# A new written-out order for all engines, with 44 constant matmuls in place of 30

## The chip, the core and the metric

The kernel runs on one NeuronCore of a Trainium2 chip. The core has five engines that work side by side, each through its own instructions in order: TensorE (PE, matmuls and transposes; its weight loads are shown apart as PEld), VectorE (DVE), ScalarE (ACT), GpSimd (POOL) and SyncE (SP, which here only issues DMA transfers). POOL issues DMA transfers too, those that convert to another type on the way. The metric is the device time of one execution in microseconds (us); lower is better.

## The reference

A block-sparse attention feeds a gated feed-forward layer. There are 4 batches, 8 heads, 768 positions and 64 dimensions; keys are cut into 24 chunks of 32, and every query keeps the 6 chunks with the highest upper bound.

```python
k_min = np.min(k_chunks, axis=3)
k_max = np.max(k_chunks, axis=3)
ub = np.sum(np.maximum(q[:, :, :, None, :] * k_min[:, :, None, :, :], q[:, :, :, None, :] * k_max[:, :, None, :, :]), axis=-1)
ub = np.where(causal, ub, -1000000000.0)
top_chunks = np.argsort(ub, axis=-1)[..., -top_k:]
scores = scale * np.matmul(q, k.transpose(0, 1, 3, 2))
scores = np.where(mask, scores, -1000000000.0)
...
attn = attn / (np.sum(attn, axis=-1, keepdims=True) + 1e-09)
return np.matmul(attn, v).astype(np.float32)
...
x = np.ascontiguousarray(attn_out.transpose(0, 2, 1, 3)).reshape(B * S, H * D)
gate = 1.0 / (1.0 + np.exp(-(x @ w_gate)))
val = x @ w_val
return (gate * val @ w_out).astype(np.float32)
```

The feed-forward layer has 512 inputs, 1536 hidden columns and 3072 tokens.

## The kernel before

**Units.** Tokens are worked in eight units of up to three blocks of 128 positions. Unit 0 holds the first block of batches 0, 1 and 2, which need no choice of chunks (they see only themselves); its three attentions are the small functions with an `f` in the name (`kfT_0`, `scf_1`, `pvf_2_0` and so on, the number being the batch). Unit 1 is blocks 1 to 3 of batch 0; units 2 to 7 follow.

**Steps of a first block** (`first`, from L699): load `k`, `q`, `v` in halves (`kf0_0`, `qf1_0`, `vf_0`, L636 and L631); transpose keys and queries on TensorE in f32 (`kfT`, `qfT`, L709); cast them to f16 (`kf16`, `qf16`, L454 on DVE, L452 on ACT); scores (`scf`, L746); two exponentials, one for each half of the heads (`expf`, ACT, L751); two causal masks on POOL (`cmf`, L753); values (`pvf`, L760, whose `v` was cast by `v16_0_0` or `vc`); reciprocal and scale on DVE (`rzf`, `xf`, L766 and L768); transpose back (`xpsf`, L775) and copy into the layer's input (`xTf`).

**Steps of unit 1** before its scores: load (`k0_u1` to `q3_u1`, L647); copy to a transposable layout (`kn`, `qn`); transpose (`kT`, `qT`, L795); chunk extremes (`kx0`, `kx1`, L681) and their difference (`kcr`, L688); copies of keys and queries into the score operands (`kt`, `hk`, `qf`, `hq`) and the clipped queries (`qm`, L695). The bounds are one group of matmuls (`ub_u1`, L896), which needs all of `kcr`, `qf` and `qm`. DVE then finds the sixth largest bound (`ubn`, `mx`, `ap`, `apt`), and `hqm` copies the resulting mask rows into the score operand. Rows of a fixed pattern (`epat`, copied by the eight `hkp`) stand opposite to them. The scores of unit 1 are `sc_u1_HEAD_BANK`.

**The layer.** `g_uN_I` and `v_uN_I` are the gate and value products of 128 hidden columns (four matmuls of 384 columns each, L1259); `tanh` (ACT) and `hg` (DVE) follow, then the output product (`o`, or the seven products `p1` to `p7` of a Strassen step, L1082). Weights come in three parts each by POOL's DMA queue with a cast from f32 to f16: `wg0` to `wg2` (L612), `wv0` to `wv2` (L613), `wo0` to `wo2` (L618). The first quarter of `wg0`'s rows is a transfer of its own, `wgp` (L610). A gate product of the first four hidden blocks reads both `wg0` and `wgp`.

**The constant matmuls.** `keep_awake` (L589 to L593) multiplies a tile of ones by itself into a PSUM bank that nobody reads. They are named `fl_0` to `fl_29`. Each writes a bank, so it takes its turn with the other users of that bank.

**What sets the order.** The functions above only describe operations. Three long strings give the rest. `ORDER` (from L96) lists all 2010 operations as `name=engine`; the kernel emits them in that order, and each engine (P, A, V, G for POOL, S for SP) runs its own in the order of the list. `SLOTS` gives the place of every rotating buffer: eight PSUM banks, six landing places for `kf`, `qf`, `vf` and the `v` loads, and so on. A transfer into a place waits until the old contents have been read. `TIES` adds waits that no data asks for: `a<b` makes `a`, always work of POOL, wait for the end of `b`, always work of DVE.

```python
        for w in ORDER.split():
            name, _, e = w.partition("=")
            op = ops[name]
            op.engine = {"P": PE, "A": ACT, "V": DVE, "G": POOL, "S": SP}[e]
...
        for b in ties.get(op.name, ()):
            tc.add_manual_dep(traced[n], ends[b], mybir.DependencyInfo(mybir.DependencyClass.Sync, mybir.DependencyReason.DATA), reason="tie")
```

Of the kernel before, what the change touches and what calls it, by code (L numbers as in the profile page):

```python
# [112 lines left out]
hk0_u1_0=A hq1_u1_1=A sc_u1_0_2=P exp_u1_0_2=A sc_u1_1_2=P sc_u1_0_1=P sc_u1_0_0=P exp_u1_1_2=A sc_u1_1_0=P sc_u1_1_1=P
exp_u1_0_0=A exp_u1_0_1=A v_u0_7=P wo0=G hqm0_u1_2=G sc_u1_2_2=P exp_u1_2_2=A sc_u1_2_0=P exp_u1_2_0=A sc_u1_3_0=P sc_u1_3_2=P
exp_u1_3_2=A exp_u1_1_0=A sc_u1_3_1=P exp_u1_3_1=A exp_u1_3_0=A v16_0_3=G wo1=G v_u0_4=P sc_u1_2_1=P v_u0_6=P exp_u1_2_1=A
hk1_u1_0=G v16_0_2=G wo2=G mx1_u1=V ap1_u1=V apt1_u1=V hqm1_u1_0=V g_u0_5=P tanh_u0_5=A v_u0_5=P exp_u1_1_1=A hqm1_u1_2=A g_u0_6=P
tanh_u0_6=A g_u0_7=P tanh_u0_7=A hg_u0_7=V v16_0_1=G cm_u1_3=G pv_u1_3=P cm_u1_2=G hk1_u1_1=G g_u0_4=P tanh_u0_4=A hg_u0_4=V
vf1_3=G hq1_u1_2=G pv_u1_2=P sc_u1_5_1=P sc_u1_4_2=P sc_u1_4_1=P rz_u1_1=V x_u1_1=V exp_u1_4_1=A v_u0_9=P v_u0_10=P xps_u1_1=P
xT_u1_1=A exp_u1_4_2=A hg_u0_6=V hk1_u1_3=V hg_u0_5=V v_u0_8=P g_u0_10=P tanh_u0_10=A kcr1=V hg_u0_10=V g_u0_8=P tanh_u0_8=A
hg_u0_8=V sc_u1_5_2=P exp_u1_5_2=A g_u0_9=P tanh_u0_9=A hg_u0_9=V sc_u1_4_0=P exp_u1_4_0=A cm_u1_1=G pv_u1_1=P cm_u1_0=G qn_u2_2=G  # L120
# [1336 lines left out]
```

## Time and profile before

| | us |
|---|---|
| Median of three runs | 281.13 |
| Lowest and highest | 280.3, 281.24 |
| The profiled execution | 279.88 |
| Its span, first to last instruction | 278.2 |
| PE busy | 269.2 |
| DVE, ACT, POOL busy | 231.2, 180.4, 163.1 |

The profile is of one execution. PE, DVE, ACT and POOL are busy times, and a busy TensorE is not TensorE at its peak, because the ends of matmuls are modelled. L numbers are lines of the kernel before. In a list in order of time each row has its start, its length, the engine, the line, the operation, what it writes and reads, and how many are merged (x); a bracket tells how long the engine stood idle before and what released it. A row of the waits has the time in total, the count and the longest. "PEclk" is the clock that TensorE was granted, and the DMA share is that of 16 engines, so that a value over 1 means that packets queue on them.

### The profile page before, as it was taken

Reading aid. Unit: us, or ns where it says so; the run is one execution under the profiler, and the core shown is the slowest. Engines: PE = TensorE matmul, PEld = TensorE weight load, DVE = VectorE, ACT = ScalarE, POOL = GpSimd, SP = SyncE. Lnnn points to the kernel's source line nnn. Section 1 sums busy time; section 2 is a strip of 40 time slices with the busy share of each in tenths; the row PEclk is TensorE's granted clock in tenths of the full one; section 3 lists DMA queues with packets and bytes.
Section 4 is the critical chain, followed back from the end, with each engine's and each line's share of the span. In section 5 each row is a group of like instructions: output and inputs, shape, how many; then the busy total and the mean of one; then the engine's idle time right before and its main releaser. Section 6 shows DMA issues by size and latency. Waiting matters only on the chain.

```text
span 278.2 us, 7566 instructions
## 1 busy us (share of the span) xinstructions
PE 269.2 (97%) x2806; PEld 189.3 (68%) x2806; DVE 231.2 (83%) x686; ACT 180.4 (65%) x386; POOL 163.1 (59%) x262
## 2 busy tenths in 40 slices
PE   5979999999999999999999999999999999999995
PEld 3755658667755666557687657776888688778684
DVE  4799747687999998796999987978889998888985
ACT  6388969569858944468689979988983422341430
POOL 5797744639372873534669966724766467163440
PEclk9999999999999999999999999999999999999999
DMA  6999999999999598696896230100320033000304
GB/s 157 258 281 204 207 217 208 220 179 202 187 217 189 142 183 188 145 161 125 164 157 114 68 85 17 40 0 3 73 77 2 1 83 127 2 1 2 151 2 152
DMA packets 131717, 34.70 MB, mean 125 GB/s; under 512 B 119776, under 2 KB 128736, under 8 KB 131680
## 3 DMA queue, kind: packets, MB, share of 16 engines
q1 hardware_dynamic: 126912, 29.50, 50.6%
q0 software_dynamic: 4768, 4.72, 10.1%
q8 instruction: 22, 0.36, 0.5%
q14 instruction: 15, 0.12, 0.1%
HBM read 30.67 MB, written 6.29 MB: 133 GB/s over the span
## 4 chain that ended last, share of the span: by engine, by line
PE 87%; DMA 6%; DVE 5%; SPq 1%; issue 0%; POOL 0%; DVEq 0%
PE v_u L1259 20%; PE g_u L1259 15%; PE sc_u L957 12%; PE o_u L1308 11%; PE p_u L1082 10%; PE pv_u L990 7%; DMA wg<-in_moe_w_gate_dram 5%; PE p_g_u L1191 5%; PE ube_u L896 3%; DMA kf<-in_k_dram 1%; DVE xf L768 1%; PE kfT L709 1%; PE qfT L709 1%; PE fl L591 1%; DVE kx_u L681 1%; DVE kcr L681 1%
## 5 line engine op out<-in xcount | busy, mean ns | idle before, releaser
L968 ACT ACTIVATE att_u<-sc_u 128x512 f16<-128x512 f32 (+3 forms) x184 | 86.9, 573 | 8.6 <-PE sc_u L957 7.3
L1259 PE MATMUL v_u<-xT_u,wv 128*128 128x384 f16 x384 | 72.4, 326 | 0.0
L1280 DVE SCALAR_TENSOR_TENSOR hg_u<-gate_u,v_u 128x384 f16<-128x384 f16 x96 | 51.2, 545 | 19.3 <-ACT gate_u L1271 9.7
L1271 ACT ACTIVATE gate_u<-g_u 128x384 f16<-128x384 f32 x72 | 35.1, 499 | 40.3 <-PE g_u L1259 35.1
L1259 PE MATMUL g_u<-xT_u,wg 128*128 128x384 f16 x288 | 56.0, 326 | 0.9 <-ACT xT_u L452 0.5
L1259 PEld LDWEIGHTS <-wv 128*128 128x128 f16 x384 | 36.2, 98 | 20.3 <-issue 0.2
L974 POOL TENSOR_SCALAR_AFFINE_SELECT att_u<-att_u 128x384 f16<-128x384 f16 (+1 forms) x56 | 28.0, 509 | 37.4 <-ACT att_u L968 16.4
L1259 PEld LDWEIGHTS <-wg 128*128 128x128 f16 x288 | 26.7, 98 | 18.3 <-DMA wg<-in_moe_w_gate_dram 1.8
L1308 PE MATMUL o_u<-wo,hg_u 128*128 128x512 f16 x144 | 34.3, 379 | 0.0
L990 PE MATMUL pv_u<-v,att_u 128*128 128x65 f16 x640 | 26.3, 193 | 0.0
L990 PEld LDWEIGHTS <-att_u 128*128 128x128 f16 x640 | 24.2, 98 | 2.9 <-issue 0.6
L1228 DVE TENSOR_TENSOR f_g_u<-p_g_u,f_g_u 128x192 f32<-128x192 f32 (+1 forms) x72 | 24.9, 383 | 1.0 <-PE p_g_u L1191 0.4
L957 PE MATMUL sc_u<-hqe,hke 128*128 128x128 f16 (+2 forms) x220 | 25.1, 243 | 0.0
L957 PE MATMUL sc_u<-hqo,hko 128*128 128x128 f16 (+2 forms) x220 | 24.1, 243 | 0.0
L1308 PEld LDWEIGHTS <-hg_u 128*128 128x128 f16 x144 | 13.7, 98 | 13.4
L957 PEld LDWEIGHTS <-hke 128*128 128x128 f16 x220 | 16.5, 98 | 4.9 <-issue 0.6
L957 PEld LDWEIGHTS <-hko 128*128 128x128 f16 x220 | 16.4, 98 | 4.4
L673 POOL CAST v<-v 128x512 f16<-128x512 f32 x23 | 14.4, 627 | 5.8 <-DVE qf_u L863 1.8
L1271 ACT ACTIVATE gate_u<-f_g_u 128x384 f16<-128x384 f32 x24 | 11.9, 519 | 5.6 <-DVE hg_u L1280 2.9
L1011 DVE TENSOR_TENSOR x_u<-pv_u,rz_u 128x384 f16<-128x384 f32 (+1 forms) x28 | 14.6, 524 | 0.9 <-DMA xT_u<-x_u 0.6
L919 DVE MAX8 mx_u<-ubn_u 128x8 f32<-128x8 f32 (+16 forms) x152 | 12.7, 158 | 0.3
L1099 DVE SCALAR_TENSOR_TENSOR sw<-p_u,sw 128x256 f32<-128x256 f32 (+1 forms) x20 | 10.6, 528 | 2.4 <-PE p_u L1082 2.0
(187 smaller groups left out, 504.9 us busy)
## 6 DMA issues: line engine op xcount, KB each, us to landing
v<-in_v_dram SPq DMA_DIRECT2D x23, 256.0 KB, 4.7
k<-in_k_dram SPq DMA_DIRECT2D x12, 384.0 KB, 5.4
q<-in_q_dram SPq DMA_DIRECT2D x12, 384.0 KB, 5.9
out_dram<-osb_u SPq DMA_DIRECT2D x12, 256.0 KB, 3.3
out_dram<-sw SPq DMA_DIRECT2D x8, 256.0 KB, 2.1
wv<-in_moe_w_val_dram POOLq DMA_DIRECT2D x3, 512.0 KB, 9.8
wo<-in_moe_w_out_dram POOLq DMA_DIRECT2D x3, 512.0 KB, 17.6
qf<-in_q_dram SPq DMA_DIRECT2D x8, 128.0 KB, 3.3
```

Source lines behind the costliest of these rows:

```text
L673: plan.add(f"v16_{b}_{ib}", {POOL: pool(H * D)}, lambda e: nc.gpsimd.tensor_copy(v16[b % 2][:, ib, :, 0:D], at(t)), reads=[t], writes=[("v ...
L957: nc.tensor.matmul(at(t)[:, o:o + 128 * m], hk[b % 2][e_][:, p, 128 * jb:128 * jb + 128], hq[u.side][e_][:, p, 128 * x:128 * (x + m)], sta ...
L968: plan.add(f"exp_{u.name}_{h}_{y}", {ACT: act(n)}, lambda e, t=t, att=att, b0=b0, n=n: nc.scalar.activation(at(att)[:, b0:b0 + n], at(t), ...
L974: nc.gpsimd.affine_select(out=dv, in_=dv, compare_op=ALU.is_ge, fill=0.0, base=0, pattern=[[0, u.m], [1, 128]], channel_multiplier=-1)
L990: nc.tensor.matmul(at(pv)[:, last, x, :], at(att)[:, c:c + 128], v16[b % 2][:, jb, h, :], start=(jb == 0), stop=(jb == ib))
L1011: plan.add(f"x_{u.name}_{p}", {DVE: dve(u.t)}, lambda e: nc.vector.tensor_tensor(at(x_).rearrange("p a (e d) -> p e a d", e=2), at(pv)[:, ...
L1082: nc.tensor.matmul(at(to)[:, side], a(j)[:, i], b(j)[:, i], start=j == i == 0, stop=j == 2 and i == 1)
L1228: plan.add(f"{p}_{name}", {POOL: pool2(192 * n), DVE: dve(192 * n)} if slow else {DVE: dve(192 * n)}, lambda e: both(e).tensor_tensor(dst( ...
L1259: nc.tensor.matmul(at(t), w16[:, c, 128 * fb:128 * fb + 128], at(u.xt)[:, c, :], start=(c == 0), stop=(c == 3))
L1271: plan.add(f"tanh_{u.name}_{fb}", {ACT: act(T, not seven[0])}, lambda e, gv=gv, gate=gate: nc.scalar.activation(at(gate), gv(), AF.Tanh, s ...
L1280: plan.add(f"hg_{u.name}_{fb}", {DVE: dve(T)}, lambda e, vv=vv, gate=gate, hg=hg, fb=fb: nc.vector.scalar_tensor_tensor(at(hg)[:, fb % 2], ...
L1308: nc.tensor.matmul(at(o), at(hgs[fc // 2])[:, fc % 2, 128 * tb:128 * tb + 128], wo16[:, fc, lo:hi], start=(fc == 0), stop=(fc == NFB - 1))
```

## The change

The three strings are replaced. The same operations are done, with 14 constant matmuls more (`fl_30` to `fl_43`); none is taken out. 100 operations go to another engine (for instance `kn_u1_2` from ACT to DVE, `hkf0` from POOL to ACT, `vc_2` from POOL to ACT, `qm_u1_1` from ACT to POOL, `kn_u1_0` from DVE to POOL). By engine the list had 701 operations for TensorE, 385 for ACT, 540 for DVE, 256 for POOL and 128 for SP; it has 715, 396, 541, 244 and 128. 800 buffers have another place. `TIES` has 118 entries for 137. The functions are the same but for the count of the constant matmuls.

In the new order 35 of the constant matmuls come ahead of TensorE's first transpose and nine between `kfT_0` and `scf_0`; before, nine came first and 21 stood here and there up to `qT_u1_2`. On POOL the pattern `epat` comes ahead of `ident`, and `wgp` follows `wg0` and the two `cmf_2` where it used to precede both; `wv1`, `wg1`, `wv2` and `wg2` follow `wv0` without other work between. On TensorE `scf_2` comes ahead of the two `pvf_1`. From unit 1's scores on, the order on each engine is another one too, though units follow each other as before.

The start of `ORDER`, up to `ub_u1`, and the count:

```diff
-ident=G ones16=V fl_4=P fl_2=P fl_8=P fl_3=P fl_1=P fl_0=P fl_29=P k2_u1=S kn_u1_2=A qf1_0=S kf1_0=S kf0_0=S fl_6=P fl_5=P epat0=V
-ident16=V ap0=V epat=G hkp110=A hkp000=A hkp001=V kT_u1_2=P kcr0=V kt_u1_2=V hk0_u1_2=G vf1_1=G hkp011=V hkp010=G vf1_2=G hkp100=G
-kf1_2=S kf0_1=S kfT_0=P kxf1=V fl_17=P fl_10=P fl_7=P kx0_u1_2=V kf16_0=V qf0_0=S qfT_0=P qf16_0=V qf1_1=S kf1_1=S kfT_1=P
-kf16_1=V fl_15=P fl_16=P scf_0=P expf_0_1=A fl_19=P qf0_1=S qfT_1=P hq0=V ap1=V fl_14=P fl_9=P fl_13=P fl_11=P fl_18=P fl_12=P
-qf16_1=V scf_1=P v10=G vf_0=S v16_0_0=G qf0_2=S qf1_2=S kf0_2=S expf_0_0=A cmf_0_0=G pvf_0_0=P rzf_0_0=V xf_0_0=V kx1_u1_2=V
-cmf_0_1=G wgp=G kfT_2=P pvf_0_1=P qfT_2=P qf16_2=V rzf_0_1=V xf_0_1=V kxf0=V expf_1_0=A cmf_1_0=G vf_1=S vc_1=G pvf_1_0=P
-rzf_1_0=V xpsf_0_0=P expf_1_1=A cmf_1_1=G pvf_1_1=P hkf0=G hk1_u1_2=A kf16_2=A scf_2=P expf_2_1=A expf_2_0=A k0_u1=S kn_u1_0=V
-kT_u1_0=P xf_1_0=V fl_20=P fl_21=P wg0=G q3_u1=S qn_u1_3=A q2_u1=S rzf_1_1=V xf_1_1=V xpsf_1_1=P hq1=V xTf_1_1=V kx0_u1_0=V
-kx1_u1_0=V vf_2=S wv0=G cmf_2_0=G fl_23=P xpsf_0_1=P fl_24=P fl_22=P fl_27=P xpsf_1_0=P vc_2=G xTf_1_0=V pvf_2_0=P rzf_2_0=V
-xf_2_0=V q1_u1=S k3_u1=S kn_u1_3=G kT_u1_3=P hkp111=A q0_u1=S fl_28=P kx1_u1_3=V cmf_2_1=G pvf_2_1=P xpsf_2_0=P rzf_2_1=V xf_2_1=V
-qT_u1_3=P qf_u1_3=V k1_u1=S qn_u1_1=A qT_u1_1=P xTf_0_0=A xTf_0_1=A qn_u1_2=A qn_u1_0=A kn_u1_1=G kT_u1_1=P kx1_u1_1=V kx0_u1_1=V
-kt_u1_0=A qm_u1_3=A fl_25=P xpsf_2_1=P fl_26=P qT_u1_2=P v_0_3=S v_0_2=S v_0_1=S qf1_3=S k0_u2=S q2_u2=S k1_u2=S qf_u1_1=V
-qf_u1_2=V v11=G wv1=G wg1=G hq0_u1_3=G qT_u1_0=P kt_u1_3=A hk0_u1_3=G hq1_u1_3=G wv2=G xTf_2_1=A xTf_2_0=A qf_u1_0=A qm_u1_0=A
-g_u0_0=P g_u0_2=P kx0_u1_3=V kcr_f=V kcr_u1=V hkp101=V hq1_u1_0=V hkf1=V kt_u1_1=V hk0_u1_1=G wg2=G qm_u1_2=A qm_u1_1=A ub_u1=P
-ubn0_u1=V ubm0_u1=V hq0_u1_1=A hq0_u1_2=A g_u0_3=P g_u0_1=P mx0_u1=V ap0_u1=V apt0_u1=V hqm0_u1_0=V v_u0_1=P v_u0_0=P v_u0_2=P
...
+ones16=V fl_30=P fl_13=P fl_23=P qf0_0=S fl_6=P fl_7=P fl_43=P fl_9=P fl_15=P fl_36=P epat0=V epat=G hkp011=A hkp100=V vf1_2=G
+v10=G ident=G ident16=V hkp110=A k2_u1=S qf1_0=S kf0_1=S kn_u1_2=V kcr0=V hkp001=V fl_1=P fl_17=P fl_0=P fl_5=P fl_42=P fl_39=P
+fl_31=P fl_3=P fl_19=P fl_20=P fl_2=P fl_37=P fl_10=P fl_32=P fl_34=P fl_35=P fl_4=P fl_26=P fl_25=P fl_18=P fl_14=P fl_33=P
+fl_12=P fl_8=P fl_41=P fl_38=P vf1_1=G hkp000=G kT_u1_2=P kt_u1_2=V kf0_0=S qfT_0=P qf16_0=V kf1_0=S kfT_0=P kf16_0=A fl_29=P
+fl_27=P fl_22=P fl_11=P fl_28=P fl_16=P fl_21=P fl_40=P fl_24=P hkp010=V scf_0=P hq0=V kxf0=V kf1_1=S vf_0=S v16_0_0=G kfT_1=P
+kf16_1=V qf0_1=S qf1_1=S qfT_1=P qf16_1=V qf0_2=S qf1_2=S expf_0_1=A cmf_0_1=G pvf_0_1=P rzf_0_1=V xf_0_1=V expf_0_0=A hk0_u1_2=A
+cmf_0_0=G pvf_0_0=P rzf_0_0=V xf_0_0=V kx1_u1_2=V scf_1=P expf_1_0=A cmf_1_0=G xpsf_0_1=P expf_1_1=A kf1_2=S kf0_2=S kfT_2=P
+q2_u1=S kf16_2=A vf_1=S qfT_2=P qf16_2=V ap1=V kx0_u1_2=V xpsf_0_0=P xTf_0_0=A scf_2=P vc_1=G pvf_1_0=P rzf_1_0=V xf_1_0=V
+cmf_1_1=G pvf_1_1=P rzf_1_1=V xf_1_1=V xpsf_1_1=P kxf1=V xpsf_1_0=P xTf_1_0=V k0_u1=S kn_u1_0=G kT_u1_0=P kx1_u1_0=V kx0_u1_0=V
+ap0=V wg0=G expf_2_0=A cmf_2_0=G expf_2_1=A cmf_2_1=G qn_u1_2=A wgp=G vf_2=S vc_2=A pvf_2_0=P q3_u1=S qn_u1_3=A k3_u1=S kn_u1_3=V
+pvf_2_1=P rzf_2_1=V rzf_2_0=V qT_u1_3=P kT_u1_3=P xf_2_1=V xpsf_2_1=P wv0=G q0_u1=S qn_u1_0=A v_0_3=S q1_u1=S xf_2_0=V xpsf_2_0=P
+hq1=V kx1_u1_3=V xTf_1_1=A hkp111=A wv1=G wg1=G kx0_u1_3=V hkp101=V qT_u1_0=P qf_u1_0=V wv2=G k1_u1=S kn_u1_1=V qn_u1_1=A hkf0=A
+xTf_2_1=A qf_u1_3=A hk1_u1_2=A xTf_0_1=A qm_u1_3=A xTf_2_0=A qT_u1_2=P qf_u1_2=A hq1_u1_3=A qm_u1_0=A wg2=G hq1_u1_0=G kcr_f=G
+qT_u1_1=P qf_u1_1=V qm_u1_1=G kT_u1_1=P kx1_u1_1=V kx0_u1_1=V kcr_u1=V kt_u1_1=V hk0_u1_1=V qm_u1_2=A kt_u1_3=A hq0_u1_3=A
+kt_u1_0=A g_u0_2=P g_u0_3=P tanh_u0_3=A hk0_u1_3=A wo0=G hq0_u1_1=G wo1=G hk0_u1_0=G hq0_u1_2=G ub_u1=P ubn0_u1=V ubm0_u1=V
+ubn1_u1=V mx0_u1=V ap0_u1=V apt0_u1=V hqm0_u1_2=G g_u0_0=P g_u0_1=P tanh_u0_0=A v_u0_2=P tanh_u0_2=A hg_u0_2=V hq0_u1_0=A v_u0_1=P
+tanh_u0_1=A hg_u0_1=V v_u0_0=P hg_u0_0=V v_u0_3=P hg_u0_3=V hqm0_u1_0=A sc_u1_3_2=P exp_u1_3_2=A sc_u1_0_2=P exp_u1_0_2=A
...
-    for i in range(30):
+    for i in range(44):
         keep_awake(i)
```

And the start of `TIES`:

```diff
-hqm0_u1_2<hqm0_u1_0 v16_0_3<hg_u0_1 hk1_u1_0<ubm1_u1 v16_0_2<hg_u0_2 v16_0_1<hqm1_u1_0 cm_u1_1<hk1_u1_3 qn_u2_2<kcr1
...
+v16_0_3<hkf1 cm_u1_3<mx1_u1 cm_u1_2<apt1_u1 cm_u1_0<hg_u0_4 hk1_u1_0<hg_u0_5 hq1_u1_2<rz_u1_1 cm_u1_1<x_u1_1 cm_u1_5<xT_u1_1
...
```

More of the change, by code (lines that the diff above doesn't have):

```diff
@@ L113 @@
[L113 to L120, printed above, removed]
@@ L269 @@
-vf_0:5 kf_1:3 qf_1:4 vf_1:0 kf_2:2 qf_2:1 vf_2:3 kq_u1:0 v_0_1:2 v_0_2:5 v_0_3:4 kfT_0:2 kf16_0:3 kx_f:0 qfT_0:6 qf16_0:4
-scf_0_0:4 scf_0_1:5 attf_0_0:1 pvf_0_0:5 rzf_0_0:0 xf_0_0:0 xpsf_0_0:5 xT_u0:0 attf_0_1:2 pvf_0_1:6 rzf_0_1:1 xf_0_1:1 xpsf_0_1:1
-kfT_1:7 kf16_1:5 qfT_1:0 qf16_1:6 vh_1:1 scf_1_0:7 scf_1_1:3 attf_1_0:3 pvf_1_0:7 rzf_1_0:0 xf_1_0:2 xpsf_1_0:7 attf_1_1:1
-pvf_1_1:3 rzf_1_1:1 xf_1_1:0 xpsf_1_1:0 kfT_2:4 kf16_2:4 qfT_2:0 qf16_2:0 vh_2:2 scf_2_0:1 scf_2_1:0 attf_2_0:3 pvf_2_0:0
@@ L273 @@
-rzf_2_0:0 xf_2_0:0 xpsf_2_0:7 attf_2_1:2 pvf_2_1:2 rzf_2_1:1 xf_2_1:1 xpsf_2_1:2 kn_u1_0:5 kT_u1_0:4 kx_u1:1 kt_u1_0:1 kn_u1_1:1
-kT_u1_1:5 kt_u1_1:0 kn_u1_2:0 kT_u1_2:1 kt_u1_2:0 kn_u1_3:1 kT_u1_3:3 kt_u1_3:2 qn_u1_0:5 qT_u1_0:6 qf_u1:0 qm_u1:0 qn_u1_1:0
-qT_u1_1:0 qn_u1_2:4 qT_u1_2:1 qn_u1_3:6 qT_u1_3:6 ube_u1:0 ubo_u1:7 ubn_u1:0 mx_u1:0 apt_u1:0 g_u0_0:4 gate_u0_0:0 v_u0_0:5
-hg_u0_0:0 g_u0_1:1 gate_u0_1:3 v_u0_1:3 g_u0_2:2 gate_u0_2:1 v_u0_2:0 hg_u0_1:1 g_u0_3:6 gate_u0_3:2 v_u0_3:2 g_u0_4:1 gate_u0_4:0
@@ L351 @@
[L351 removed]
+epat:0 fl_0:3 fl_1:1 fl_2:3 fl_3:0 fl_4:1 fl_5:4 fl_6:3 fl_7:4 fl_8:0 fl_9:6 fl_10:5 fl_11:1 fl_12:7 fl_13:1 fl_14:5 fl_15:7
+fl_16:6 fl_17:2 fl_18:4 fl_19:1 fl_20:2 fl_21:7 fl_22:0 fl_23:2 fl_24:4 fl_25:3 fl_26:2 fl_27:7 fl_28:2 fl_29:6 fl_30:0 fl_31:7
+fl_32:6 fl_33:6 fl_34:7 fl_35:0 fl_36:0 fl_37:4 fl_38:2 fl_39:6 fl_40:0 fl_41:1 fl_42:5 fl_43:5 kf_0:2 qf_0:0 vf_0:3 kf_1:1 qf_1:4
+vf_1:2 kf_2:0 qf_2:5 vf_2:3 kq_u1:0 v_0_1:4 v_0_2:0 v_0_3:1 kfT_0:5 kf16_0:4 kx_f:1 qfT_0:4 qf16_0:3 scf_0_0:1 scf_0_1:2
@@ new lines @@
+attf_0_0:1 pvf_0_0:4 rzf_0_0:1 xf_0_0:1 xpsf_0_0:4 xT_u0:0 attf_0_1:2 pvf_0_1:0 rzf_0_1:0 xf_0_1:0 xpsf_0_1:6 kfT_1:6 kf16_1:5
+qfT_1:7 qf16_1:6 vh_1:2 scf_1_0:2 scf_1_1:1 attf_1_0:3 pvf_1_0:7 rzf_1_0:0 xf_1_0:2 xpsf_1_0:3 attf_1_1:1 pvf_1_1:4 rzf_1_1:1
+xf_1_1:0 xpsf_1_1:0 kfT_2:7 kf16_2:1 qfT_2:0 qf16_2:3 vh_2:0 scf_2_0:2 scf_2_1:1 attf_2_0:2 pvf_2_0:2 rzf_2_0:1 xf_2_0:0
+xpsf_2_0:1 attf_2_1:3 pvf_2_1:1 rzf_2_1:0 xf_2_1:1 xpsf_2_1:3 kn_u1_0:5 kT_u1_0:7 kx_u1:0 kt_u1_0:0 kn_u1_1:5 kT_u1_1:4 kt_u1_1:1
@@ new lines @@
+kn_u1_2:1 kT_u1_2:3 kt_u1_2:0 kn_u1_3:3 kT_u1_3:5 kt_u1_3:2 qn_u1_0:2 qT_u1_0:0 qf_u1:0 qm_u1:0 qn_u1_1:0 qT_u1_1:3 qn_u1_2:6
+qT_u1_2:2 qn_u1_3:1 qT_u1_3:4 ube_u1:1 ubo_u1:3 ubn_u1:0 mx_u1:0 apt_u1:0 g_u0_0:2 gate_u0_0:2 v_u0_0:6 hg_u0_0:1 g_u0_1:5
+gate_u0_1:3 v_u0_1:7 g_u0_2:0 gate_u0_2:0 v_u0_2:4 hg_u0_1:0 g_u0_3:6 gate_u0_3:1 v_u0_3:1 g_u0_4:2 gate_u0_4:0 v_u0_4:3 hg_u0_2:2
+g_u0_5:6 gate_u0_5:3 v_u0_5:1 g_u0_6:6 gate_u0_6:1 v_u0_6:0 hg_u0_3:3 g_u0_7:4 gate_u0_7:2 v_u0_7:5 g_u0_8:2 gate_u0_8:3 v_u0_8:6
```

478 lines of the change are left out of this document (239 added, 239 removed).

## The prediction

> **What bounds the kernel now.** I read the busy totals first, then the stretches, then TensorE's own waits, then each engine in order of time for the first 30 us.
>
> ```profile
> PE 269.2 (97%) x2806; PEld 189.3 (68%) x2806; DVE 231.2 (83%) x686; ACT 180.4 (65%) x386; POOL 163.1 (59%) x262
> 14.00:18.00 4.00, 2.39 (x32) 1.65 (x31) 3.65 (x12) 2.83 (x6) 4.00 (x7) 1.00 1.14 298
> 22.00:30.00 8.00, 7.37 (x70) 3.89 (x69) 7.19 (x28) 6.09 (x16) 5.17 (x9) 1.00 1.22 203
> 50.00:100.00 50.00, 50.00 (x545) 33.06 (x542) 44.17 (x126) 38.76 (x87) 30.14 (x54) 1.00 1.02 190
> PE kT_u L795 <- POOL epat L566: 0.8, 1, 0.8
> ...
> PE g_u L1259 <- DMA wg<-in_moe_w_gate_dram: 0.2, 1, 0.2
> ```
>
> TensorE is 97% busy. The rows of stretches give length, then busy time of PE, PEld, DVE, ACT, POOL, then clock, DMA share and GB/s. From 50 us on there is nothing to win by order alone: 50.00 of 50.00. What is left lies in front: 14 to 18 us shows TensorE with 1.6 us of holes while POOL and DVE are full or close to it and the 16 DMA engines are over-subscribed (share 1.14, and still 1.22 up to 30 us). After 25.75 us TensorE waits once, 0.2 us, for gate weights. So the end moves as the start of the first gate products moves (the first `g_u`, L1259).
>
> ```profile
> 1.12 2.10 PE L591 MATMUL fl<-ones 128*128 128x256 f16 x9 [1.12 <-DVE ones L587]
> 5.81 1.09 PE L709 MATMUL kfT<-ident,kf 128*128 128x128 f32 x4 [0.90 <-DMA kf<-in_k_dram]
> 9.85 0.61 PE L746 MATMUL scf<-qf,kf 64*128 64x128 f16 x8
> 10.39 0.40 PE L591 MATMUL fl<-ones 128*128 128x256 f16 x1
> 10.58 1.06 PE L709 MATMUL qfT<-ident,qf 128*128 128x128 f32 x4
> 12.43 0.40 PE L746 MATMUL scf<-qf,kf 64*128 64x128 f16 x8
> 12.89 0.63 PE L709 MATMUL kfT<-ident,kf 128*128 128x128 f32 x4
> 15.70 0.40 PE L746 MATMUL scf<-qf,kf 64*128 64x128 f16 x8
> 17.65 0.27 PE L591 MATMUL fl<-ones 128*128 128x256 f16 x1
> 17.87 0.49 PE L591 MATMUL fl<-ones 128*128 128x256 f16 x3
> 22.82 1.76 PE L1259 MATMUL g_u<-xT_u,wg 128*128 128x384 f16 x8 [0.51 <-ACT xT_u L452]
> 24.51 0.45 PE L896 MATMUL ube_u<-qf_u,kcr 64*32 64x320 f32 x1
> 25.75 1.47 PE L1259 MATMUL g_u<-xT_u,wg 128*128 128x384 f16 x8
> ```
>
> Start, length, shape, count. The clock column shows 1.00 throughout, but the same four transposes cost 1.06 us at 10.58 and 0.63 us at 12.89: TensorE ran at half pace until about 11.6 us. A constant matmul takes (2.10 - 0.40) / 8 = 0.21 us early and (0.49 - 0.27) / 2 = 0.11 us late. Eight `g_u` took 1.76 us at 22.82 and 1.47 us at 25.75: the first eight lost 0.29 us inside, on weights.
>
> **The constant matmuls.** 14 are added; the new order puts 35 at the very front, nine between `kfT_0` and `scf_0`, none later. At the early pace 35 last 7.4 us (to 8.6), at the late pace 3.9 (to 5.0). TensorE's unbroken stretch before began at 5.81 and turned fast 5.8 us later; from 1.12 that gives 6.9, so 27 slow ones and eight fast: to 7.8. I take 7.8. `kT_u1_2`, at 4.04 before, then waits for nothing but these: Pool now makes `ident` after the pattern.
>
> ```profile
> 0.79 0.20 POOL masks.py:197 MEMSET ident<- 128x128 f32 x1 [0.29 <-POOLq L1441]
> 1.93 2.04 POOL L566 TENSOR_SCALAR_AFFINE_SELECT epat<-epat 32x768 f16<-32x768 f16 x2 [0.56 <-DVE epat L561]
> 12.82 0.79 POOL L610 DMA_DIRECT2D wg<-in_moe_w_gate_dram  x1
> 14.77 0.64 POOL L753 TENSOR_SCALAR_AFFINE_SELECT attf<-attf 128x512 f16<-128x512 f16 x1
> 15.91 0.80 POOL L612 DMA_DIRECT2D wg<-in_moe_w_gate_dram  x1
> 16.70 0.78 POOL L613 DMA_DIRECT2D wv<-in_moe_w_val_dram  x1
> 18.08 0.62 POOL L456 CAST vh<-vf 128x512 f16<-128x512 f32 x1
> 18.64 0.51 POOL L456 COPY kn_u<-kq_u 128x384 f32<-128x384 f32 x1
> 20.39 0.76 POOL L613 DMA_DIRECT2D wv<-in_moe_w_val_dram  x1
> 23.36 0.75 POOL L613 DMA_DIRECT2D wv<-in_moe_w_val_dram  x1
> 28.73 0.72 POOL L456 COPY hqe<-apt_u 64x640 f16<-64x640 f16 x1 [1.07 <-DVE hqe L454]
> DMA to landing us min/median/max: 5.5/5.5/5.5
> DMA to landing us min/median/max: 7.3/12.0/14.2
> DMA to landing us min/median/max: 9.5/9.8/13.5
> ```
>
> The last three rows are the times from issue to landing of the lines L610 (`wgp`), L612 (`wg0` to `wg2`) and L613 (`wv0` to `wv2`). The pattern ends at 3.97; two small fills and `ident` bring Pool to about 5.0, and DVE's `ident16` and `kn_u1_2` (that copy takes Pool 0.51) to about 5.8. The fillers to 7.8 hide this; without them it would cost the 1.8 us from 4.04. The transposes `kT_u1_2`, `qfT_0`, `kfT_0` (11 at 0.11) and nine fillers (1.0) put `scf_0` at 10.0, against 9.85. So the fast pace buys back what the fillers took, no more. By the same spacing `scf_1` stands at 12.6 (12.43 before) and `qfT_2` ends at 14.2.
>
> **Second block, ACT and DVE.** Rows of SP's queue, ACT and DVE:
>
> ```profile
> 8.41 0.51 SPq L636 DMA_DIRECT2D kf<-in_k_dram  x1
> 16.20 1.08 ACT L751 ACTIVATE attf<-scf 128x512 f16<-128x512 f32 x2 [1.12 <-PE scf L746]
> 23.19 1.19 ACT L695 ACTIVATE qm_u<-qf_u 128x320 f32<-128x320 f32 x3
> 14.23 0.69 DVE L454 CAST qf<-qfT 128x512 f16<-128x512 f32 x1
> 23.71 0.21 DVE L688 TENSOR_TENSOR kcr<-kx_u,kcr 128x48 f32<-128x48 f32 x1
> ```
>
> Before, `scf_2` stood behind both `pvf_1` and ran at 15.70. Now it is ahead of them, and starts after DVE's cast `qf16_2` (0.69 us): 14.9, so 0.8 earlier. The loads of block 2 now wait on SP for `qfT_0` to free a landing buffer, to about 8.6; behind them stand all loads of unit 1. Before, the last of block 2 was issued at 8.41, so that 0.8 us is their cover, and late loads would eat it. ACT did 16 instructions from 17.28 to 24.38 (0.44 each). The new order has 18 there (it gains `vc_2`, `hkf0`, `hk1_u1_2`, `hq1_u1_3` and one `qf`, and gives up two `kt` and one `qm`), 8.0 us from 16.4: 24.4. DVE has 26 instructions from the end of `qf16_2` to `kcr_u1` in both orders, 9.0 us: 23.9 again. So `ub_u1` is released when it was (24.51), and TensorE could start gate products at 22.7, behind `kT_u1_1`. One price is unknown: `qm_u1_1` on Pool, where the trace has no clipping by Pool. Nearest row: the copy `kn_u`, 0.51 us; the dearest would be the pattern's 1.0 us a piece. I take 0.6; it ends by 24.5 either way, beside gate products.
>
> **What is late next: the first weights.** This is my main term. The chain of work that ended last has `wg2` from issue to landing, and 24 products in a row:
>
> ```profile
> 26.18 14.22 DMA wg<-in_moe_w_gate_dram
> ...
> 259.25 3.90 PE v_u L1259 x24
> ```
>
> `g_u0_2` needs `wgp` (the first quarter, 128 KB) as well as `wg0`. Before, `wgp` was issued at 12.82 and landed 5.5 us later, at 18.3; `wg0` at 15.91 landed 7.3 later, at 23.2. Now Pool issues `wg0` after `kn_u1_0`, and `wgp` only behind the two masks of block 2. Walk: `expf_1_0` ends at 13.6; two masks, `vc_1`, `kn_u1_0` (0.64, 0.64, 0.62, 0.51): `wg0` at 16.0. Issue 0.80, two masks 1.28: `wgp` at 18.1. It cannot land before 18.1 + 5.5 = 23.6. `wg0` is due at 16.0 + 7.3 = 23.3, and 128 KB behind it cost 1.6 at the rate of the old `wg0` (384 KB in 23.2 - 18.3 = 4.9), 0.9 at that of the last ones (512 KB from 36.9, where `wv2` lands 13.5 after 23.36, to 40.4, where `wg2` lands). I take 24.2, between 23.6 and 24.9. The eight gate products then end at 24.2 + 1.47 = 25.67, against 24.58: **+1.1 us**, where the bounds give +0.5 and +1.8, and -0.4 if weights land before 22.7.
>
> **Later weights and the rest.** Pool issues `wg2` some five us earlier, but from 16.7 us the weights queue is never empty, so it moves with `wgp`, about +1; its 0.2 us wait stays. `wv0` (9.5 after 16.70: 26.2) goes to 27.2 and is wanted at 28.0: 24.2, `ub_u1` 1.24 (24.51 to 25.75) and four groups of products at 0.65 (3.90 / 6). The redrawn waits of Pool, the PSUM places and the order of the body I cost at nothing, hidden under full TensorE; were it no longer covered, the front's own holes (4.00 - 2.39 = 1.6 us in one stretch) are the upper end, and the lower end is -0.5: that 0.2 us wait and one hidden loss of 0.29.
>
> **Sum.** Span 278.2 + 1.1 = 279.3. The profiled execution took 279.88, 1.68 around the span, hence 281.0; the median shown, 281.13, is 1.25 above that execution. On the median: 282.2.
>
> **Rivals.** *A, faster.* TensorE is fast much sooner, and the front moves up: say to 6.4, half-way between 7.8 and the 5.0 of all-fast fillers, 1.4 earlier. Pool's issues follow, `wgp` to 16.7, landing at 22.2 by its own 5.5; the eight products end at 23.67, 0.9 ahead, and the 0.2 us wait goes: 280.0. For it: nothing but constants is needed to keep TensorE busy, and the 0.63 against 1.06 is there to be had. Against it: before, pace rose only after 5.8 us without a gap. [...] *N, no change.* The same early end, but the queue behind `wg0` rules: 24.2 - 1.4 = 22.8, products end at 24.27, 0.3 ahead: 280.8. *B, slower.* The fillers stay slow to their end, 8.6 instead of 7.8: 283.0. *C, slower still.* By Pool's order and these landings never more than six weight loads were in flight; at `wo1` it is seven now. If Pool holds `wo1` until `wv1` has landed (20.39 + 9.8 + 1.0 = 31.2), then its issue (0.75), two copies (0.5 each) and the mask copy `hqm0_u1_2` (0.72) release `sc_u1_3_2`, the first scores, at 33.7. They are wanted at 30.6 (28.0 and four groups of `v`): 3.1 more, 285.3. Against it: the sixth was issued as fast as the first.
>
> **How the numbers follow.** Forecast 0.32, A 0.27, N 0.15, B 0.13, C 0.08, a body that stalls in some other place 0.05. A change under 0.3% (0.84 us) can't be told from none here. Faster: A but for 0.02, and 0.03 of N: 0.28. Same: 0.02 of A, 0.10 of N, 0.06 of the forecast's low end: 0.18. Slower: the rest, 0.54. The range goes from just under A (less 0.2, part of the body's low end) to B plus 1.2 (most of the body's upper end): 279.8 to 284.2. It leaves out C at its full price and the ends of the others, about 0.2. The forecast alone spans 281.6 to 282.9.
>
> **What would show it.** In the new trace: fillers ending near 7.8 (A: 6.4; B: 8.6); `scf_2` near 14.9; the first `g_u` idle on the weights' DMA near 24.2, not on `xT_u`; `ub_u1` right behind its products; no wait of TensorE after 26 us beyond 0.3. First `g_u` before 22.5 refutes me, and so does a gapped body.

## The result, and the profile after

| | before | after |
|---|---|---|
| Median | 281.09 (12 runs) | 283.58 (12 runs) |
| Lowest and highest | 280.3, 283.26 | 281.37, 284.59 |
| Ratio, 95% interval | | 1.0076, 1.0049 to 1.0103 |
| The profiled execution, its span | 279.88, 278.2 | 282.69, 281.0 |
| Mean granted clock of that execution | 1.000 | 0.987 |
| Start of the second pair of `g_u` | 25.75 | 28.50 |
| From there to the end of the span | 252.45 | 252.50 |

The change is slower, by 0.8% (0.5 to 1.0%). Medians are of all runs, while the ratios leave out slow ones, those over 1.5% above the fastest of their kernel. The profiled execution of the kernel before is not one of its twelve runs and lies under the lowest of them. Line numbers of the changed kernel are two lower than before, and those of the kernels below differ by a few. Its busy total and TensorE's first 30 us, in order of time:

```profile
PE 271.5 (97%) x2820; PEld 190.9 (68%) x2820; DVE 234.2 (83%) x687; ACT 187.3 (67%) x397; POOL 151.0 (54%) x250
1.11 5.43 PE L589 MATMUL fl<-ones 128*128 128x256 f16 x35 [1.11 <-DVE ones L585]
6.38 0.49 PE L793 MATMUL kT_u<-ident,kn_u 128*128 128x128 f32 x3
...
7.58 1.18 PE L589 MATMUL fl<-ones 128*128 128x256 f16 x9
8.70 0.40 PE L744 MATMUL scf<-qf,kf 64*128 64x128 f16 x8
...
11.31 0.40 PE L744 MATMUL scf<-qf,kf 64*128 64x128 f16 x8
...
13.79 0.40 PE L744 MATMUL scf<-qf,kf 64*128 64x128 f16 x8 [0.67 <-DVE qf L452]
...
21.45 0.55 PE L793 MATMUL qT_u<-ident,qn_u 128*128 128x128 f32 x3 [0.47 <-ACT xT_u L450]
23.23 0.52 PE L793 MATMUL kT_u<-ident,kn_u 128*128 128x128 f32 x3 [1.23 <-ACT qm_u L693]
24.25 2.47 PE L1257 MATMUL g_u<-xT_u,wg 128*128 128x384 f16 x8 [0.50 <-DMA wg<-in_moe_w_gate_dram]
26.64 0.74 PE L894 MATMUL ube_u<-qf_u,kcr 64*32 64x320 f32 x1
...
28.50 1.48 PE L1257 MATMUL g_u<-xT_u,wg 128*128 128x384 f16 x8
```

In these two profiles the whole loss lies in the front: the second pair of gate products is 2.75 us later, the span 2.8 longer, and what follows takes 252.5 us in both. The reader should follow two things in these rows. The front is ahead at 13.79 (`scf_2`, at 15.70 before) and behind at 24.25, with three holes just in front of the first `g_u`: 0.47, 1.23 and 0.50. Then the eight `g_u` take 2.47 us where the same eight take 1.48 at 28.50, and `ub_u1` takes 1.86 (26.64 to 28.50) where it took 1.24.

The second is the clock. The stretches of the changed kernel, cut where the granted clock changed (length, then busy time of PE, PEld, DVE, ACT, POOL, then clock, DMA share, GB/s):

```profile
14.33:17.74 3.41, 1.87 (x24) 1.22 (x22) 3.28 (x10) 2.39 (x5) 3.35 (x6) 1.00 1.08 293
17.74:21.15 3.41, 3.20 (x16) 2.28 (x15) 3.37 (x11) 3.11 (x6) 3.41 (x6) 0.50 1.13 219
21.15:24.56 3.41, 1.38 (x8) 0.83 (x9) 2.35 (x5) 3.30 (x9) 1.97 (x4) 1.00 1.18 193
24.56:27.97 3.41, 3.41 (x32) 1.40 (x37) 1.48 (x4) 2.68 (x7) 3.07 (x6) 0.50 1.21 197
27.97:31.38 3.41, 3.41 (x34) 1.77 (x19) 2.58 (x16) 1.64 (x4) 0.00 (x0) 1.00 1.22 203
```

Read the PE column against the clock of the row below it: 1.87 busy of 3.41, then a stretch at 0.50; 3.20, then 1.00; 1.38, then 0.50; 3.41, then 1.00. In this profile the holes before the first `g_u` are paid twice, once as idle time and once as half a clock over the 3.41 us that follow, on which the gate products and the bounds fall. Who made the holes stands in the rows of POOL, ACT and DVE, with the landing time of L608 (`wgp`):

```profile
14.99 1.00 POOL L610 DMA_DIRECT2D wg<-in_moe_w_gate_dram  x1
17.17 0.59 POOL L608 DMA_DIRECT2D wg<-in_moe_w_gate_dram  x1
23.64 1.02 POOL L695 TENSOR_SCALAR qm_u<-qf_u 128x320 f32<-128x320 f32 x1 [0.99 <-DVE qf_u L452]
25.92 0.76 POOL L616 DMA_DIRECT2D wo<-in_moe_w_out_dram  x1
DMA to landing us min/median/max: 7.0/7.0/7.0
16.99 0.51 ACT L450 COPY qn_u<-kq_u 128x384 f32<-128x384 f32 x1 [0.78 <-DMA kq_u<-in_q_dram]
18.04 0.51 ACT L450 COPY qn_u<-kq_u 128x384 f32<-128x384 f32 x1 [0.54 <-DMA kq_u<-in_q_dram]
24.38 0.83 ACT L693 ACTIVATE qm_u<-qf_u 128x320 f32<-128x320 f32 x2
22.53 0.55 DVE L452 COPY kn_u<-kq_u 128x384 f32<-128x384 f32 x1 [0.82 <-DMA kq_u<-in_k_dram]
```

`wgp` was issued at 17.17 and landed at 24.2, and that released the first `g_u`. The hole of 1.23 us before `kT_u1_1` is put down to an ACT `qm_u`, which that transpose doesn't read; its own input is DVE's `kn_u1_1`, done at 23.08, and that copy waited for the load `k1_u1`. So two of the three holes are transfers that came late.

### The profile page after: what moved, and what is told of

The parts are those of the page before. It is cut to its first block, busy times and chain, and to the rows that moved or that the text cites. A ratio compares the mean times of both kernels' runs of the same rounds, so it can differ in the third digit from the quotient of the medians.

```text
span 281.0 us, 7590 instructions
## 1 busy us (share of the span) xinstructions
PE 271.5 (97%) x2820; PEld 190.9 (68%) x2820; DVE 234.2 (83%) x687; ACT 187.3 (67%) x397; POOL 151.0 (54%) x250
## 4 chain that ended last, share of the span: by engine, by line
PE 93%; DMA 3%; DVE 2%; POOL 1%; issue 0%; ACT 0%; DVEq 0%
PE v_u L1257 22%; PE g_u L1257 17%; PE sc_u L955 13%; PE o_u L1306 11%; PE p_u L1080 8%; PE pv_u L988 7%; PE p_g_u L1189 5%; PE ube_u L894 3%; DMA wg<-in_moe_w_gate_dram 3%; PE fl L589 2%; DVE ox L1097 1%; POOL attf L751 1%; PE kfT L707 1%; PE scf L744 1%; PE qfT L707 0%; PE kT_u L793 0%
## 5 line engine op out<-in xcount | busy, mean ns | idle before, releaser
L1278 DVE SCALAR_TENSOR_TENSOR hg_u<-gate_u,v_u 128x384 f16<-128x384 f16 x96 | 50.6, 545 | 19.6 <-ACT gate_u L1269 12.8
L1257 PE MATMUL g_u<-xT_u,wg 128*128 128x384 f16 x288 | 57.6, 331 | 0.5 <-DMA wg<-in_moe_w_gate_dram 0.5
L972 POOL TENSOR_SCALAR_AFFINE_SELECT att_u<-att_u 128x384 f16<-128x384 f16 (+1 forms) x56 | 28.0, 507 | 26.4 <-ACT att_u L966 13.6
L955 PE MATMUL sc_u<-hqo,hko 128*128 128x128 f16 (+2 forms) x220 | 25.7, 243 | 0.0
L955 PE MATMUL sc_u<-hqe,hke 128*128 128x128 f16 (+2 forms) x220 | 24.5, 244 | 0.0
```

What stands on the lines that cost most here:

```text
L955: nc.tensor.matmul(at(t)[:, o:o + 128 * m], hk[b % 2][e_][:, p, 128 * jb:128 * jb + 128], hq[u.side][e_][:, p, 128 * x:128 * (x + m)], sta ...
L972: nc.gpsimd.affine_select(out=dv, in_=dv, compare_op=ALU.is_ge, fill=0.0, base=0, pattern=[[0, u.m], [1, 128]], channel_multiplier=-1)
L1257: nc.tensor.matmul(at(t), w16[:, c, 128 * fb:128 * fb + 128], at(u.xt)[:, c, :], start=(c == 0), stop=(c == 3))
L1278: plan.add(f"hg_{u.name}_{fb}", {DVE: dve(T)}, lambda e, vv=vv, gate=gate, hg=hg, fb=fb: nc.vector.scalar_tensor_tensor(at(hg)[:, fb % 2], ...
```

## The experiments

All run against the kernel before, whose median was 281.03 to 281.15 in these comparisons; a kernel has twelve runs unless six are named, and one profile. "Second pair" is the start of the second pair of `g_u` in the profile, as above. In the diffs a list is cut to the operations moved.

**wgp early.** The prediction's main term undone in the changed kernel.

```diff
-cmf_1_0=G ... wg0=G expf_2_0=A cmf_2_0=G expf_2_1=A cmf_2_1=G qn_u1_2=A wgp=G
+wgp=G cmf_1_0=G ... wg0=G expf_2_0=A cmf_2_0=G expf_2_1=A cmf_2_1=G qn_u1_2=A
```

> The changed kernel with wgp issued ahead of cmf_1_0 as before, nothing else. Theory (two losses: first weights late, and TensorE throttled to half pace between 17.7 and 28 us because its holes have no filler): the first gate products start near 23.7 instead of 24.25, now behind kT_u1_1; the granted clock still falls below 1.0 before 30 us; about -0.5 us, 283.0. Rival (the late first weights are the whole loss): back to about 281.5.

Measured: 284.06, ratio 1.0065 (1.0027 to 1.0103). No gain. TensorE in its profile, which is of one of the fastest of the twelve runs (281.65):

```profile
22.78 0.90 PE L793 MATMUL qT_u<-ident,qn_u 128*128 128x128 f32 x3 [0.39 <-ACT xT_u L450]
23.50 0.61 PE L793 MATMUL kT_u<-ident,kn_u 128*128 128x128 f32 x3
24.82 1.46 PE L1257 MATMUL g_u<-xT_u,wg 128*128 128x384 f16 x8 [0.71 <-ACT xT_u L450]
```

The wait for weights is gone and the first `g_u` is no earlier: it waits for ACT's copies into the layer's input instead. In this execution the clock was low from 16.9 to 23.7 us, so the products themselves ran at full pace. What made the runs about the median 2.4 us longer than this one is not in it. By the medians, late weights alone don't explain the loss.

**28 constant matmuls later.** They were to keep the clock up. 6 behind `pvf_1_1`, 2 behind `kT_u1_0`, 2 behind `pvf_2_0`, 6 behind `qT_u1_0`, 10 behind `qT_u1_1`, 2 behind `kT_u1_1`.

```diff
+fl_44=P ... fl_71=P
...
-    for i in range(44):
+    for i in range(72):
```

> The changed kernel with 28 more constant matmuls in TensorE's holes between pvf_1_1 and g_u0_2; wgp stays late. Theory: granted clock 1.00 throughout, first gate products still at about 24.2 on the weights' DMA, then 1.47 us for eight and 1.24 for ub_u1 in place of 2.47 and 1.9: -1.6 us, 282.0. Rival (the clock falls for another reason, or the fillers only stand in the way): 283.6 or more.

**Both of these.**

> Both edits. Theory: the gains add up, -2.1 us, 281.5, within 0.3% of the kernel before. Rival (something else in the redrawn order or the engines' shares costs time): at least 1 us above the kernel before.

Measured: 282.89, ratio 1.0066 (1.0034 to 1.0099), and 282.87, 1.0073 (1.0038 to 1.0107). The clock stayed at 1.000 in both profiles and the eight `g_u` took 1.46 us, but they started at 25.29 and 26.09, because the added matmuls stood in the way. The first median lies between its theory and its rival; the second, 1.8 us above the kernel before, is as its rival had it. TensorE in the first of the two kernels:

```profile
19.86 1.90 PE L593 MATMUL fl<-ones 128*128 128x256 f16 x6
21.82 0.88 PE L797 MATMUL qT_u<-ident,qn_u 128*128 128x128 f32 x6
22.53 1.68 PE L593 MATMUL fl<-ones 128*128 128x256 f16 x10
```

Six in one bank took 1.90 us, ten in two banks 1.68. What was given to the clock was taken from the transposes, so these two tell little of the clock's price.

**The same from the other side.** The kernel before without its nine constant matmuls after `scf_2`.

```diff
-fl_20=P fl_21=P fl_23=P fl_24=P fl_22=P fl_27=P fl_28=P fl_25=P fl_26=P
```

> The kernel before without its nine constant matmuls after scf_2 (21 left). Theory: TensorE is throttled in the holes between 14 and 24 us, granted clock below 1.0 in 14 to 28 us, and +1 to +2 us, 282 to 283. Rival (the fillers there do nothing for the clock): 281.1, clock 1.000.

Measured: 280.98, ratio 0.9990 (0.9964 to 1.0015). The theory missed. The clock did fall, and the median lost nothing:

```profile
17.00:20.00 3.00, 2.01 (x15) 1.60 (x16) 2.14 (x7) 2.98 (x7) 2.71 (x5) 0.50 1.19 304
20.00:23.50 3.50, 3.50 (x23) 3.44 (x22) 2.62 (x7) 2.75 (x8) 3.23 (x7) 0.50 1.23 208
23.50:27.00 3.50, 3.50 (x48) 1.74 (x47) 3.42 (x11) 3.10 (x8) 1.00 (x3) 0.99 1.22 204
```

Half a clock between 17 and 23.5 us falls on transposes; TensorE was full in the second of these stretches, and the clock was back when `g_u` began. In this profile the second pair is at 26.31, 0.56 later than in the profile before, while the medians agree. That the transposes have slack there, since ACT, DVE and the loads set the pace, is argued and not shown; if so, a low clock costs only where TensorE's own pace sets the end.

**15 constant matmuls, better placed.** In the changed kernel: 3, 2, 2, 1, 1, 4, 2, behind `pvf_1_1`, `kT_u1_0`, `pvf_2_0`, `xpsf_2_0`, `qT_u1_0`, `qT_u1_1`, `kT_u1_1`, in banks free there. Then with `wgp` early too; then with the 256 KB load `v_0_3` behind the last loads of unit 1 as well; then with copies moved off ACT's and DVE's path. The expectations call these four kernels c1 to c4.

```diff
+fl_44=P ... fl_58=P
...
-cmf_2_1=G qn_u1_2=A wgp=G
+wgp=G cmf_1_0=G
...
-v_0_3=S q1_u1=S ... k1_u1=S
+q1_u1=S ... k1_u1=S v_0_3=S
...
-xTf_1_1=A hkp111=A ... kx0_u1_3=V hkp101=V ... hkf0=A ... hk1_u1_2=A ... hq1_u1_3=A ... hk0_u1_1=V qm_u1_2=A
+xTf_1_1=A ... kx0_u1_3=V ... hk0_u1_1=V hkp101=V qm_u1_2=A hkf0=A hk1_u1_2=A hq1_u1_3=A hkp111=A
```

> The new order with 15 constant matmuls more between pvf_1_1 and kT_u1_1, never more than four in one place and spread over free banks, and nothing else. Theory (a slow clock at the first products costs 1.6 us, late weights 1.1): clock 1.000, first g_u still on the weights at about 24.2, its eight in 1.5 us, ub_u1 in 1.24, second g_u pair at 26.9 instead of 28.5, median about 282.0. Rival (the constant matmuls push the transposes, as 28 of them did): first g_u at 25 or later, second pair near 27.9, median 282.9.

> The same 15 constant matmuls, and wgp ahead of cmf_1_0 as in the first experiment. Theory: the weights are there at 18.3, and the next bound is ACT's last copy into the layer's input (xTf_2_0, 23.4 to 24.8 in the runs so far): first g_u at 23.5 to 24.5, second pair at 26.2 to 27.2, median 281.0 to 282.2. Rival (both together save nothing, since ACT and the loads of unit 1 hold the transposes): as c1, 282 to 283.

> As c2, with the 256 KB load v_0_3 on SP behind q1_u1 and k1_u1 instead of ahead of them. Theory (late loads of unit 1 starve ACT, 1.3 us of waits for q in the changed kernel, and DVE, 0.8): q1 and k1 land 0.6 to 1 us sooner, ACT's copies move with them, first g_u at 22.9 to 23.6, second pair 25.7 to 26.4, median 280.5 to 281.2. Rival (16 DMA engines are full anyway, so order among loads moves nothing): as c2.

> As c3, with four copies on ACT (hkp111 of 1.47 us, hkf0, hk1_u1_2, hq1_u1_3 of some 0.5 each) behind qm_u1_2, and hkp101 on DVE behind hk0_u1_1. Theory (ACT's queue is the bound once clock, weights and loads are mended): xTf_2_0 and the last qm up to 2.5 us sooner on ACT, first g_u at 22.3 to 22.9 behind kT_u1_1, ub_u1 right behind it, second pair 25.0 to 25.7, median 279.8 to 280.5, under both kernels. Rival (DVE and the loads set kT_u1_1 and kcr_u1): as c3 within 0.4.

| added to the changed kernel | median | ratio, 95% interval | second pair |
|---|---|---|---|
| nothing | 283.58 | 1.0076, 1.0049 to 1.0103 | 28.50 |
| 15 matmuls | 283.58 (6 runs) | 1.0104, 1.0077 to 1.0132 | 31.52 |
| and `wgp` early | 281.89 | 1.0044, 1.0025 to 1.0063 | 27.33 |
| and `v_0_3` behind | 281.67 | 1.0023, 0.9989 to 1.0057 | 27.01 |
| and ACT, DVE relieved | 281.56 | 1.0027, 1.0007 to 1.0047 | 26.16 |

The 15 matmuls alone gained nothing, and missed their theory and their rival. Nor did a full clock alone: three of the six runs had a mean clock of 0.998 to 1.000 and took 283.19 to 283.61. The profile is of the slowest of the six (285.69, clock 0.988), and shows what can go wrong there on ACT and then on TensorE:

```profile
23.86 0.51 ACT L452 COPY qn_u<-kq_u 128x384 f32<-128x384 f32 x1 [3.64 <-DMA kq_u<-in_q_dram]
25.21 0.90 PE L795 MATMUL qT_u<-ident,qn_u 128*128 128x128 f32 x3 [3.89 <-ACT xT_u L452]
```

ACT stood 3.64 us for the load `q1_u1`, which was issued at 16.00 behind `v_0_3`, amid the weights. With `wgp` early as well, the interval lies wholly under that of the 15 alone (281.89 against 283.58), the first `g_u` starts at 24.70 with nothing but TensorE's own queue ahead, and the clock is 1.000. Its median is where its theory had it. The next two steps moved the second pair the way that was expected, by 0.3 and 0.85 us, but not as far (27.01 for 25.7 to 26.4, 26.16 for 25.0 to 25.7), and the medians by 0.2 and 0.1, which can't be told from nothing: both theories missed, and both rivals came. For the last kernel the profile gives a reason:

```profile
26.16 1.47 PE L1259 MATMUL g_u<-xT_u,wg 128*128 128x384 f16 x8
...
34.73 0.82 PE L1259 MATMUL g_u<-xT_u,wg 128*128 128x384 f16 x4 [0.34 <-DMA wg<-in_moe_w_gate_dram]
...
42.01 0.82 PE L1259 MATMUL g_u<-xT_u,wg 128*128 128x384 f16 x4 [0.76 <-DMA wg<-in_moe_w_gate_dram]
```

From the second pair to the end it took 254.1 us, not 252.5: TensorE, ready sooner, now waits for `wg1` and `wg2`, 1.1 us of the 1.6. The profile of the step before has no such wait, so its median stays without a reason.

**Unit 2's loads held back**, to give those weights room.

```diff
-v_0_2=S ... k0_u2=S ... k1_u2=S ... q2_u2=S ... v_0_4=S
+v_0_2=S ... q2_u2=S v_0_4=S k0_u2=S ... k1_u2=S
```

> As c4, with the loads of unit 2 (all but q2_u2) held back on SP until about 32.6 us instead of 20.3: v_0_4 is put ahead of them, whose landing place is free when POOL's cast v16_0_3 has read v_0_3. Theory (the DMA engines are full, and c4 gave its earlier front back in 1.1 us of waits for wg1 and wg2): both waits go, the time from the second pair of gate products to the end falls from 254.1 to 252.5, median 280.0 to 280.6, under both kernels. Rival (unit 2's loads are not what is in the way, or are then late themselves): waits stay or come back at unit 2's copies, median 281.5 or more.

Measured: 287.28 (6 runs), ratio 1.0232 (1.0197 to 1.0267). The theory missed. The two waits for weights are gone from the profile, which the theory had right, but SP stood until 33.63 and unit 2 paid:

```profile
33.63 0.37 SPq L667 DMA_DIRECT2D v<-in_v_dram  x1
46.50 0.41 ACT L452 COPY kn_u<-kq_u 128x256 f32<-128x256 f32 x1 [3.56 <-DMA kq_u<-in_k_dram]
47.35 0.66 PE L990 MATMUL pv_u<-v,att_u 128*128 128x65 f16 x9 [3.30 <-ACT gate_u L1271]
```

ACT waited 3.56 us for a key load, and behind that copy stood the `gate_u` for which TensorE waited 3.30. That the weights and SP's loads share what is short fits this; a smaller step was not tried.

**Loads without wgp.** The 15 matmuls and `v_0_3` behind, but `wgp` late. It differs by `wgp` alone from the kernel of the table's row "and `v_0_3` behind".

> As c1 (15 constant matmuls in the later front), with v_0_3 behind q1_u1 and k1_u1 on SP, and wgp left late. Theory (c1 lost its gain to q1_u1, 3.6 us of waiting on ACT behind v_0_3's transfer): that wait falls under 1.5, first g_u waits for the weights alone at about 24.2, second pair at 26.9 to 27.2, median 281.6 to 282.2. Rival (wgp late among the other weights is what holds the loads of unit 1 up): as c1, 283 or more.

Measured: 283.16 (6 runs), ratio 1.0100 (1.0061 to 1.0139), against 1.0023 (0.9989 to 1.0057) with `wgp` early. Its profile (283.35, near its median), TensorE:

```profile
22.75 0.55 PE L795 MATMUL kT_u<-ident,kn_u 128*128 128x128 f32 x3
...
25.66 1.47 PE L1259 MATMUL g_u<-xT_u,wg 128*128 128x384 f16 x8 [2.15 <-DMA wg<-in_moe_w_gate_dram]
```

With clock and loads mended TensorE stands 2.15 us before the weights: `wgp` landed at 25.6, 1.4 later than in the changed kernel. It was issued 0.7 later, at 17.9, and took 0.7 more, perhaps because the loads of unit 1 had gone ahead. This is the clearest reading of the main term: late `wgp` is worth 1.5 us in the medians (283.16 less 281.67), or 0.8% by the two ratios, whose intervals lie just apart. The theory's median, 281.6 to 282.2, was missed, and the rival's number came, but not by the rival's mechanism: ACT did not wait for `q1_u1` in this profile, so late `wgp` does not hold that load up here. What stood in its place is the wait for `wgp` itself, 2.15 us where the theory had the first `g_u` at 24.2.

**wgp late in the kernel before**, alone and then together with the removal of its nine late constant matmuls.

```diff
-cmf_0_1=G wgp=G kfT_2=P ... wg0=G
+cmf_0_1=G kfT_2=P ... wg0=G wgp=G
```

> The kernel before with wgp right behind wg0 on POOL, and nothing else: the prediction's main term alone. By it wgp is issued at 16.7 instead of 12.8 and cannot land before 22.2, more likely 23.6 to 24.3 behind wg0; the first eight g_u end at 25.1 to 25.8 instead of 24.58, second pair 0.5 to 1.2 later, median 281.6 to 282.3. Rival (wg0 then lands sooner by what wgp gave up, and the two together as before): within 0.3 of before.

> The kernel before with both: wgp right behind wg0 (alone 281.58 against 281.15) and without the nine constant matmuls after scf_2 (alone 280.98 against 281.09). Theory (the two losses multiply: TensorE idles 1 to 2 us for the weights, the next window of the granted clock is half pace, and it falls on the first gate products and the bounds): first eight g_u 2 us or more instead of 1.47, ub_u1 1.5 or more, median 282.4 to 283.2, most of what the new order lost. Rival (the losses add): g_u at 1.5 us behind the weights, median 281.3 to 281.7.

Measured: 281.58, ratio 1.0021 (1.0000 to 1.0042), and 281.63, ratio 1.0015 (0.9989 to 1.0040). The wait is there in the first one's profile, on TensorE:

```profile
24.54 1.47 PE L1259 MATMUL g_u<-xT_u,wg 128*128 128x384 f16 x8 [1.84 <-DMA wg<-in_moe_w_gate_dram]
27.19 1.47 PE L1259 MATMUL g_u<-xT_u,wg 128*128 128x384 f16 x8
```

Its second pair stands 1.44 later than in the profile before, its median 0.43 higher, just under the forecast. With both edits the theory that the losses multiply fell. The clock was 0.988 in the profile, and low before `g_u` rather than on it (TensorE 3.41 of 3.41 busy from 20.09 to 23.50, at 0.50, then 1.00), the eight products took 1.47 us, and the median lies where the losses add. In that profile they did not meet: transposes at half pace kept TensorE at work until 23.99, `wgp` landed at 24.1, and the first `g_u` came at 24.11 without a hole.

## Why the prediction was right, and where not

The median, 283.58, lies in the range and on the side that had most of the chance, 1.4 above the predicted 282.2. Against the profiled execution, on which the sum was made: a span of 279.3 was predicted, 281.0 measured. Of the 2.75 us by which the second pair came later, 1.43 is the later start of the first `g_u` (1.38 forecast, 24.2 for 22.82); the other 1.32 is the slower products and bounds behind it, where the forecast had a gain of 0.29. The lost clock was costed at nothing, so that the median still fell into the range is in part luck.

- **Only the front matters; the first `g_u` sets the end; the body at nothing.** Right here: 252.45 and 252.50 us after the second pair. The kernel that moved the front to 26.16 shows how far it reaches: there the body stalled, on weights.
- **35 matmuls to 7.8.** Wrong for this execution. They ended at 6.54 (1.11 and 5.43). The step that failed is "from 1.12 that gives 6.9", which counted 5.8 us of unbroken work until TensorE turns fast. The stretches of these matmuls alone show it at 4.09, 3.0 us after the first:

```profile
1.11:4.09 2.98, 2.98 (x15) 2.12 (x16) 1.00 0.59 150
4.09:6.43 2.34, 2.34 (x22) 1.95 (x20) 1.00 1.04 233
```

 15 in 2.98 us is 0.20 each, 22 in 2.34 is 0.11. That was rival A's early pace (6.4). But the place differs from one execution to the next: in the profiles of the experiments on the changed kernel, whose first 35 matmuls are the same, these end between 6.45 and 8.01. The latest, with ACT and DVE relieved:

```profile
1.12 6.89 PE L591 MATMUL fl<-ones 128*128 128x256 f16 x35 [1.12 <-DVE ones L587]
```

 So the step took as one fixed time what the runs show to vary by 1.6 us. `scf_0`, `scf_1` and `scf_2` came 1.3, 1.3 and 1.1 sooner than predicted. A's consequence did not follow: its 0.9 us gain needed `wgp` at 22.2.
- **POOL's walk and the weights at 24.2.** Landing was hit to the tenth, by two errors against each other: `wgp` was issued 0.9 sooner than the walk gave (17.17 for 18.1) and took 7.0 us, not the 6.1 that the forecast amounts to. The first `g_u` idled on the weights' DMA, as the test demanded.
- **"The eight gate products then end at 24.2 + 1.47."** This is the step that failed in size. They took 2.47, and `ub_u1` behind them 1.86 instead of 1.24: 1.6 us together, all but 0.1 of what the span was off. The prediction had TensorE fast for good once it was warm, and didn't ask what holes of its own forecast would do to the clock.
- **The price of late `wgp`, +1.1.** Its sign holds where it shows. Its size depends on what else is late: to undo it gained nothing in the changed kernel as it stands (the first experiment); it is 1.5 us where clock and loads are mended, and 0.43 in the kernel before, where the interval of the ratio begins at 1.0000.
- **Loads of unit 1, cover 0.8.** I looked at the wait for `qfT_0` and not at `v_0_3`, which the new order puts ahead of `q1_u1` and `k1_u1`. The waits that came (ACT 0.78 and 0.54, DVE 0.82) made ACT's `qm` end at 25.21 for 24.4 and `kT_u1_1` wait 1.23.
- **`qm_u1_1` on POOL at 0.6.** It took 1.02, the dear end of the bounds, hidden beside `g_u`. **Rival C** fell: `wo1` was issued at 25.92 in 0.76 us and POOL was not held.

What the medians show: the late first weights cost 1.5 to 1.7 us once the 15 matmuls are in (two pairs of kernels whose intervals lie apart, the second pair barely). With `wgp` late the 15 matmuls gained nothing (283.58 to 283.58); with `wgp` early they took 284.06 to 281.89, but the intervals of these two ratios overlap. It looks as if either loss, mended alone, left the other or a third to fill its place; both mended gave 1.7 us of the 2.5.

What they don't show: that the low clock costs 1.6 us. This is read from one profile. All twelve runs of the changed kernel had a mean clock between 0.976 and 0.994, none reached 1.000; the kernel before, over the 98 runs of these comparisons, had 0.997 or more in 46, at a median of 281.02, between 0.990 and 0.997 in 31, at 280.98, and less in 21, at 281.35. The remaining 0.5 us of the best of these kernels over the one before is not settled. Its 1.1 us of waits for `wg1` and `wg2` point to the order of the transfers. No kernel here is shown to beat the one before.
